# A delta-rule attention and two gated layers on one core: from the third step on, two pairs of small matmul groups are written as one

## The chip, the cores and the metric

The kernel runs on one core of a Trainium2 chip. A core has a matrix engine (TensorE, in the profile PE, with its weight loads as PEld), VectorE (DVE), ScalarE (ACT), GpSimd (POOL) and SyncE (SP, which here only issues DMAs). Each engine runs its own instructions in order, and semaphores tie the engines together. The metric is the device time of one execution in microseconds (us). TensorE's clock is granted by the chip at one of two levels, 2.4 and 1.2 GHz; the profile shows the granted share (1.00 or 0.50, between them where a stretch holds both).

## What is computed

Three layers in a row, all in fp32. The first is a recurrence over 768 positions for 4 x 8 heads of width 48, the second a gated layer (3072 tokens, 384 to 1536 and back), the third sends each token to one of 8 experts. Cut to what matters:

```
for t in range(S):                                   # attention, S = 768
    kt, vt, bt = k_n[:, :, t], v[:, :, t], beta[:, :, t, None]
    y[:, :, t] = einsum('bhd,bhde->bhe', q[:, :, t], state)
    v_old = einsum('bhde,bhd->bhe', state, kt)
    state = state + bt * einsum('bhd,bhe->bhde', kt, vt - v_old)
xn = x / sqrt(mean(x * x) + 1e-6) * rms_g            # second layer
x = (silu(xn @ w_gate) * (xn @ w_val)) @ w_out
e_idx = argmax(x @ gate)                             # third layer: one expert per token
out = gate_w * eom * (relu(x[mask] @ w1[e]) @ w2[e])
```

## The kernel before

**Attention in steps.** The 768 positions are six steps `m` = 0 to 5 of 128, each of two chunks `ch` of 64. The 32 heads are 16 pairs, in two groups `g` of 8 pairs; a step has 32 problems of the form "one head pair's half and one chunk" side by side. In the code the third step is `m` = 2.

`Attn.early(m)` prepares a step for all heads. Small matmuls give the products of keys by keys (`keygram`, L217, tiles `gk`), ScalarE copies them out (L220 to L224), VectorE takes the lengths of the keys into account (`norms`, L135 to L143) after GpSimd has taken square roots (`roots`, L129, tile `nrm`), and `solve` inverts 32 x 32 triangles in 31 rounds of VectorE work (L275, L279). What is left of the 64 x 64 inverse is its corner, in two steps: `corner(m, 0, b)` multiplies raw products by the inverse (L312, tiles `off.0.`), and `corner(m, 1, b)` multiplies the transposed inverse `t11` by what step 0 gave, `w` (L315, tiles `off.1.`). `b` is the half of the 32 problems: a call of `corner` is 32 matmuls of 32 x 32, which the trace counts as 64, and two ScalarE copies out of PSUM (L319 into `w`, L321 into `ng`). The order is step 0 half 0, step 0 half 1, step 1 half 0, step 1 half 1, with a yield behind each.

`Attn.late(m, g)` uses the result. `gram(m, b)` makes keys by queries (L238, tiles `gq`, 16 matmuls of 64 x 64, in the trace 32, and two masked VectorE copies, L245), twice for a group `g`, for `b` = 2g and 2g + 1. Then, for each chunk, four stages: `z` (L335, then a subtraction on VectorE, L339), `u` (L342, then four ScalarE copies, L346), `y` (L357, the output, copied by ScalarE at L362) and `s` (L368, then an addition to the state `right` on VectorE, L371). `z` of the second chunk needs the `right` of the first chunk's `s`.

**The second layer in blocks.** `Moe1.block(m, g)` takes 256 tokens through 12 slices `f`. `up(f)` is 18 fp32r matmuls of 128 x 128 weights by 256 columns into a PSUM tile `gv` (L672; two buffers), then tanh and a copy on ScalarE (L678 `th`, L680 `val`), a product on VectorE (L681), a product on GpSimd (L685), a rounding on ScalarE (L687, `h` high part) and a difference on GpSimd (L688, `h` low part). `down(f - 2)` is 6 matmuls of 400 columns (L698, `po`), which need both parts of `h`. Blocks start with the transposes `xt` (L645) of the scaled input (L634) and end with a route (L725 to L791) that writes the rows to DRAM from SP (L769, L771) and lists tokens by an indirect DMA from GpSimd (L791).

**Third layer.** After the last attention step a plan gathers tokens and weights by indirect DMAs from GpSimd (L833, L986, L993), while the last blocks of the second layer still run.

**What sets the order.** Everything above is written as generators. `Weave` runs the blocks as its main line and steps the attention in between: a generator yields a pair (`pe`, `gap`), TensorE time that it has used and the planned distance to its next turn, and the planner adds `pe` to its own clock. `early` uses `eg` as gap, 3.0 from `m` = 2 on; `late` uses `self.gap`, 3.4 there. A scheduler of the framework then fixes a static order for each engine from these priorities and its own estimate of times. So a changed yield can move instructions on all engines, those of the blocks too.

**Tiles that tie the parts together.** The small products of attention share one PSUM tag, `at`, with four buffers. `t11` lies in the SBUF tag `nb` and `w` in `xa`. The keys of the next step, `ek`, are loaded from SP into the same two tags (L204: group 0 into `nb`, group 1 into `xa`), and the squares of the keys, `sq` (L106), into `xa` and `x`. So the keys of step m + 1 can be loaded only when the last matmul of `corner(m, 1, 1)` has read `t11` and `w`.

Of the kernel before, what the change touches and what calls it, by code (L numbers as in the profile page):

```python
# [29 lines left out]
@contextmanager  # L30
def ahead(tc):

    now, tc.cur_priority = tc.cur_priority, ahead.next
    yield
    ahead.next, tc.cur_priority = tc.cur_priority, now


class Attn:
# [338 lines left out]
    def early(self, m):  # L377


        eg, slow = EGAP[min(m, 2)], SLOW[min(m, 2)]  # L380
        ready = "aT" in self.t[m]
        for g in range(2):
            self.keys(m, 0) if g == 0 else None
            if not ready:
                self.squares(m, g)
            yield 0, 1.0
        self.keys(m, 1)
        T = self.t[m]
        T["raw"] = [self.pool.tile([P, 32, 32], F32, tag=tag, name=f"{tag}r{m}") for tag in ("raw", "x")]
        n = GRAMS.get(m, 0)  # L390
        if n:
            ns = slice(0, 8 * n)
            self.nc.sync.dma_start(out=T["raw"][0][:, ns], in_=self.a["kk", m][:, 0, ns])
            for q in range(4):
                r = slice(32 * q, 32 * q + 32)
                self.nc.sync.dma_start(out=T["raw"][1][r, ns], in_=self.a["kk", m][r, q % 2, ns])
        for g in range(2):
            if 2 * g >= n:
                self.keygram(m, g)
            for b in (2 * g, 2 * g + 1):  # L400
                if not ready:
                    self.roots(m, b)
            yield (0.8 if 2 * g >= n else 0.0), 2 * eg
        if not ready:
            yield 0, 1.0
            self.norms(m)
            yield 0, 1.5
        acc = 0
        solve = self.solve(m)
        while True:  # L410
            with self.behind(m):
                t = next(solve, None)
            if t is None:
                break
            acc += t
            if acc > 0.9:
                yield 0, acc * slow
                acc = 0
        yield 0, acc * slow + 0.5
        for step, b in ((0, 0), (0, 1), (1, 0), (1, 1)):  # L420
            with nullcontext() if m else ahead(self.tc):
                self.corner(m, step, b)
            self.inverted = step == 1 and b == 1
            yield 0.7, eg
        self.solved = m

    def x(self, m, i, xs):
# [32 lines left out]
    def late(self, m, g, xs):  # L460
        T = self.t[m]
        while "aT" not in T:
            yield 0, 1.0
        for b in (2 * g, 2 * g + 1):
            if b < GRAMS.get(m, 0):
                self.mask(m, b)
            else:
                self.gram(m, b)
            yield 0.64, self.gap
        self.values(m, g)  # L470

        while self.solved < m or self.turned < 2 * m - 2 + g:
            yield 0, 1.0
        self.x(m, g, xs)
        for ch in range(2):
            for stage in "zuys":
                if stage == "s" and ch:
                    self.after(m, g, xs[m, g])
                    if m == NM - 1:
                        break  # L480
                self.chain(m, ch, g, stage)
                yield 0.64, self.gap
        if m + 1 < NM:
            for what in "Kqgvk":
                self.load(m + 1, g, what)
# [729 lines left out]
def tile_kernel(ctx: ExitStack, tc: tile.TileContext, a: dict):  # L1215
# [63 lines left out]
    for i in range(PRE):  # L1279
        next(weights)  # L1280
        if i >= GRAMS_AT:
            next(grams, None)
        if i == QUERIES_AT:
            for g in range(2):
                A.load(0, g, "q")
            for _ in range(4):
                next(late)
# [12 lines left out]
    while (0, 0) not in scales:  # L1300
        next(late)
    with ahead(tc):
        for _ in M.turn(0, 0, xs[0, 0]):
            pass
    A.turned = 0
    late = W.add(late)
    W.add(first)
    W.add(weigh(), WSTART)
# [27 lines left out]
    for m in range(NM):  # L1336
# [21 lines left out]
        if m == NM - 2:  # L1358
            for side in [route] + sides:
                W.finish(side)  # L1360
            W.until(lambda: scales[NM - 1, 1] not in W.sides)
            att_s.close()
            p1 = ctx.enter_context(tc.tile_pool(name="c1", bufs=1, side="right"))
            C = Moe2(tc, p1, ps, c, a)
            C.hi[0], C.lo[0] = (p1.tile([P, 3072], F32R, name=f"w1{i}") for i in "hl")

            def early():
                yield from C.plan_full(M.cnt)
                for i in range(2):
                    xg.append(C.gather(p1, *subs[i][1:]))  # L1370
                C.load(subs[0][0], 0)
                C.load(subs[0][0], 1)
                for i in range(2, N1):
                    xg.append(C.gather(p1, *subs[i][1:]))
                yield 0, 14.0
                for i in range(3):
                    C.split(0, i, 3)
                    yield 0, 2.5

            pre = W.add(early())  # L1380
# [103 lines left out]
```

## Time and profile before

| | us |
|---|---|
| median of 3 timed runs | 1078.29 (1073.57 to 1079.56) |
| the profiled execution, its own time | 1081.5 |
| span of the profiled execution, first to last instruction | 1079.7 |
| PE busy | 973.7 (90%), 11189 matmuls |
| PEld busy | 915.5 (85%) |
| DVE busy | 700.0 (65%) |
| ACT busy | 477.1 (44%) |
| POOL busy | 460.6 (43%) |
| mean granted clock of TensorE | 0.977 |

The time line has three parts: a start without full use of TensorE (to about 240 us), the middle, where blocks and attention steps are woven (to about 750 us), and the third layer. The changed calls lie between about 250 and 706 us. In the middle TensorE is busy nearly all the time, so the order there is read from the waits of TensorE and from the granted clock, not from the shares of the whole.

### The profile page before, as it was taken

Reading aid. Unit: us, or ns where it says so; the run is one execution under the profiler, and the core shown is the slowest. Engines: PE = TensorE matmul, PEld = TensorE weight load, DVE = VectorE, ACT = ScalarE, POOL = GpSimd, SP = SyncE. Lnnn points to the kernel's source line nnn. Section 1 sums busy time; section 2 is a strip of 40 time slices with the busy share of each in tenths; the row PEclk is TensorE's granted clock in tenths of the full one; section 3 lists DMA queues with packets and bytes.
Section 4 is the critical chain, followed back from the end, with each engine's and each line's share of the span. In section 5 each row is a group of like instructions: output and inputs, shape, how many; then the busy total and the mean of one; then the engine's idle time right before and its main releaser. Section 6 shows DMA issues by size and latency. Waiting matters only on the chain.

```text
span 1079.7 us, 27699 instructions
## 1 busy us (share of the span) xinstructions
PE 973.7 (90%) x11189; PEld 915.5 (85%) x11189; DVE 700.0 (65%) x1976; ACT 477.1 (44%) x1241; POOL 460.6 (43%) x526
## 2 busy tenths in 40 slices
PE   3825888989999999999999999997998999999993
PEld 2724787889998898989989999997998899999993
DVE  5996879849962898269945995143417756567550
ACT  6625552354345343544364334443335544355440
POOL 9608334443535343543545443346542523324210
PEclk9999999899998999999999999999999999999997
DMA  9811770121302221220222030004106544446320
GB/s 287 236 60 40 207 161 1 30 62 46 74 17 60 60 57 35 61 60 19 58 73 63 2 75 4 14 16 162 66 9 186 203 153 163 154 151 227 144 82 15
DMA packets 55433, 97.05 MB, mean 90 GB/s; under 512 B 6400, under 2 KB 41878, under 8 KB 52482
## 3 DMA queue, kind: packets, MB, share of 16 engines
q1 hardware_dynamic: 45266, 48.76, 17.6%
q0 software_dynamic: 7680, 45.08, 11.7%
q8 instruction: 90, 1.47, 0.6%
q10 hardware_dynamic: 2352, 1.37, 0.5%
q14 instruction: 45, 0.37, 0.1%
HBM read 83.78 MB, written 12.09 MB: 89 GB/s over the span
## 4 chain that ended last, share of the span: by engine, by line
PE 59%; issue 11%; DVE 10%; POOL 7%; DMA 7%; ACT 4%; POOLq 0%; SPq 0%; ACTq 0%; DVEq 0%
PE gv L672 22%; PE po L698 10%; PE cpo L1063 9%; PE ph L1042 8%; PE y L357 2%; POOL th L685 2%; DMA raw<-in_wv_dram 1%; PE gq L238 1%; POOL h L688 1%; POOL nrm L129 1%; DMA sq<-in_kv_dram 1%; POOL raw L560 1%; PE s L368 1%; DVE tmp L275 1%; PE z L335 1%
## 5 line engine op out<-in xcount | busy, mean ns | idle before, releaser
L685 POOL TENSOR_TENSOR th<-th,val 128x256 f32<-128x256 f32 x144 | 115.5, 802 | 249.0 <-DVE th L681 154.9
L698 PE MATMUL po<-wout,h 128*128 128x400 f32 x864 | 191.8, 354 | 10.7 <-POOL h L688 6.5
L681 DVE SCALAR_TENSOR_TENSOR th<-th,gv 128x256 f32<-128x256 f32 x144 | 59.9, 416 | 178.2 <-ACT val L680 167.9
L698 PEld LDWEIGHTS po<-wout,h 128*128 128x128 f32 x864 | 149.2, 190 | 15.8 <-POOL h L688 8.2
L672 PE MATMUL gv<-xh,wl 128*128 128x256 f32 x864 | 151.7, 293 | 3.4 <-DVE th L681 2.1
L672 PE MATMUL gv<-xh,wgv 128*128 128x256 f32 x864 | 147.6, 293 | 2.0 <-DVE th L681 2.0
L688 POOL TENSOR_TENSOR h<-th,h 128x256 fp32r<-128x256 f32 x144 | 110.1, 765 | 82.2 <-ACT h L687 81.6
L687 ACT ACTIVATE h<-th 128x256 fp32r<-128x256 f32 x144 | 60.0, 417 | 192.1 <-POOL th L685 191.0
L672 PEld LDWEIGHTS gv<-xh,wl 128*128 128x128 f32 x864 | 126.2, 195 | 8.6 <-DVE th L681 4.9
L672 PEld LDWEIGHTS gv<-xh,wgv 128*128 128x128 f32 x864 | 124.6, 196 | 5.0 <-DVE th L681 2.7
L1063 PE MATMUL cpo<-w2h,ch 128*128 128x384 f32 (+1 forms) x464 | 124.4, 340 | 3.4 <-ACT ch L1046 3.4
L275 DVE TENSOR_TENSOR tmp<-nb,x 128x110 f32<-128x110 f32 (+35 forms) x366 | 106.8, 331 | 3.7
L678 ACT ACTIVATE th<-gv 128x256 f32<-128x256 f32 x144 | 54.6, 379 | 107.6 <-PE gv L672 92.5
L279 DVE TENSOR_TENSOR x<-x,tmp 128x110 f32<-128x110 f32 (+35 forms) x366 | 98.7, 307 | 0.3
L1042 PE MATMUL ph<-xT,w1h 128*128 128x256 f32 (+4 forms) x528 | 95.1, 313 | 1.1 <-DVE ch L1047 0.8
L1063 PEld LDWEIGHTS cpo<-w2h,ch 128*128 128x128 f32 (+1 forms) x464 | 81.9, 183 | 5.7 <-ACT ch L1046 3.9
L1042 PEld LDWEIGHTS ph<-xT,w1h 128*128 128x128 f32 x528 | 82.4, 190 | 2.7 <-issue 1.6
L672 PE MATMUL gv<-xl,wgv 128*128 128x256 f32 x432 | 80.0, 292 | 0.6 <-DVE xl L653 0.6
L1063 PE MATMUL cpo<-w2l,ch 128*128 128x384 f32 (+1 forms) x232 | 78.1, 337 | 0.0
L672 PE MATMUL gv<-xl,wl 128*128 128x256 f32 x432 | 77.8, 289 | 0.0
L1047 DVE SCALAR_TENSOR_TENSOR ch<-ph,ch 128x512 fp32r<-128x512 f32 (+4 forms) x64 | 39.0, 611 | 45.7 <-ACT ch L1046 45.7
L672 PEld LDWEIGHTS gv<-xl,wgv 128*128 128x128 f32 x432 | 64.4, 196 | 1.7 <-DVE xl L653 1.0
(241 smaller groups left out, 1766.9 us busy)
## 6 DMA issues: line engine op xcount, KB each, us to landing
kT<-in_kqT_dram SPq DMA_DIRECT2D x24, 192.0 KB, 3.8
raw<-in_wo_dram SPq DMA_DIRECT2D x12, 384.0 KB, 7.5
left<-in_kqT_dram SPq DMA_DIRECT2D x24, 192.0 KB, 7.0
v<-in_kv_dram SPq DMA_DIRECT2D x12, 384.0 KB, 3.8
raw<-in_wg_dram SPq DMA_DIRECT2D x12, 384.0 KB, 4.0
raw<-in_wv_dram SPq DMA_DIRECT2D x12, 384.0 KB, 4.1
sq<-in_kv_dram SPq DMA_DIRECT2D x10, 384.0 KB, 4.1
ek<-in_kqT_dram SPq DMA_DIRECT2D x18, 192.0 KB, 3.6
```

The source lines that it names most:

```text
L275: nc.vector.tensor_tensor(out=t, in0=nb[:, k + 1:, k:k + 1].to_broadcast([P, n, b - a]), in1=x[:, k:k + 1, a:b].to_broadcast([P, n, b - a] ...
L279: nc.vector.tensor_tensor(out=x[:, k + 1:, a:b], in0=x[:, k + 1:, a:b], in1=t, op=ALU.add)
L672: nc.tensor.matmul(out=ps[:, gv], lhsT=self.weight(wi, cc, gv, slice(f * P, f * P + P)), rhs=xx[:, cc], start=i == 0, stop=i == 8)
L678: nc.scalar.activation(out=th, in_=ps[:, 0], func=AF.Tanh, scale=0.5)
L681: self.gate = nc.vector.scalar_tensor_tensor(out=th, in0=th, scalar=1.0, in1=ps[:, 0], op0=ALU.add, op1=ALU.mult).ins
L685: nc.gpsimd.tensor_tensor(out=th, in0=th, in1=val, op=ALU.mult)
L687: nc.scalar.activation(out=h2[:, 0], in_=th, func=AF.Copy)
L688: nc.gpsimd.tensor_tensor(out=h2[:, 1], in0=th, in1=h2[:, 0].bitcast(F32), op=ALU.subtract)
L698: nc.tensor.matmul(out=po[t], lhsT=h[:, ts], rhs=self.wo[wi][:, f], start=f == 0 and i == 0, stop=f == 11 and i == 2)
L1042: nc.tensor.matmul(out=ph[:, fl], lhsT=w1[wi][:, cc, f * P:(f + 1) * P], rhs=xt[:, xi, cc], start=i == 0, stop=i == 8)
L1047: nc.vector.scalar_tensor_tensor(out=hl, in0=ph, scalar=0.0, in1=hh.bitcast(F32), op0=ALU.max, op1=ALU.subtract)
L1063: nc.tensor.matmul(out=po[t][0:rows[t]], lhsT=hs[f // 2][:, hi, f % 2, t * P:t * P + rows[t]], rhs=w2[wi][:, f], start=f == 0 and i == 0, ...
```

## The change

From `m` = 2 on, `early` yields only behind half 1 of a corner step, with twice the TensorE time and twice the gap, and `late` yields once behind both products of a group, with twice the time and twice the gap. The calls, the tiles and the instructions are the same; the sums of the planned times are too.

```
@@ in early
             self.inverted = step == 1 and b == 1
-            yield 0.7, eg
+
+            if m < 2:
+                yield 0.7, eg
+            elif b:
+                yield 1.4, 2 * eg
@@ in late
                 self.gram(m, b)
-            yield 0.64, self.gap
+            if m < 2:
+                yield 0.64, self.gap
+        if m > 1:
+            yield 1.28, 2 * self.gap
```

Since the lines behind the edits move by four and then by seven, L672 of before is L679 of the change, and so on.

Three places show what the scheduler makes of it. First TensorE, in block (2, 1), where the corner of step 3 ends (`off310`, `off311` are halves 0 and 1 of its second step). Before:

```order
L315 MATMUL off310_5972<-w3_5820,t113_5700 32x32 x32
L672 MATMUL gv212_6007<-xh21_5808,wgv0_81 128x256 x3
L672 MATMUL gv212_6007<-xl21_5809,wgv0_81 128x256 x3
L672 MATMUL gv212_6007<-xh21_5808,wgv1_82 128x256 x3
L672 MATMUL gv212_6007<-xh21_5808,wgv0_81 128x256 x3
L672 MATMUL gv212_6007<-xl21_5809,wgv0_81 128x256 x3
L672 MATMUL gv212_6007<-xh21_5808,wgv1_82 128x256 x3
L315 MATMUL off311_6035<-w3_5820,t113_5700 32x32 x32
```

Of the change:

```order
L679 MATMUL gv211_5939<-xh21_5879,wgv1_82 128x256 x3
L315 MATMUL off310_5949<-w3_5808,t113_5690 32x32 x32
L315 MATMUL off311_5984<-w3_5808,t113_5690 32x32 x32
L679 MATMUL gv211_5939<-xh21_5879,wgv0_81 128x256 x3
L679 MATMUL gv211_5939<-xl21_5880,wgv0_81 128x256 x3
```

The two halves stand in one run, and the second half has moved ahead of the 18 matmuls of `gv212` and of half of `gv211`.

Second the queue of SP, behind the corner of step 2, in block (1, 1). `y10` are the rows of the route of block (1, 0), `ek0_3` and `ek1_3` the keys and `sq30` and `sq31` the squares for step 3. Before:

```order
L106 DMA sq31_4381<-in_kv_dram 128x768
L769 DMA rows_57<-y10_4008 128x385
L771 DMA rows_57<-y10_4008 64x385 x2
L204 DMA ek0_3_4345<-in_kqT_dram 48x8x128 x2
L106 DMA sq30_4350<-in_kv_dram 128x768
L204 DMA ek1_3_4385<-in_kqT_dram 48x8x128 x2
```

Of the change:

```order
L106 DMA sq31_4381<-in_kv_dram 128x768
L204 DMA ek0_3_4345<-in_kqT_dram 48x8x128 x2
L106 DMA sq30_4350<-in_kv_dram 128x768
L776 DMA rows_57<-y10_4008 128x385
L778 DMA rows_57<-y10_4008 64x385 x2
L204 DMA ek1_3_4385<-in_kqT_dram 48x8x128 x2
```

The loads of `ek0_3` and `sq30` have moved ahead of the rows.

Third GpSimd at the end of the middle part, in block (5, 0): `lt_f` reads the list of tokens, `wraw` are weights of the third layer, `xg` its gathered rows, `th504` to `h506` belong to slices 4 to 6 of the block. Before:

```order
L833 DMA lt_f_10552<-list_60,li_f_10550 6x128
L685 TENSOR_TENSOR th504_10714<-th504_10714,val504_10716 128x256
L993 DMA wraw0_10480<-in_w1_dram,wi_f_10626 128x3072
L993 DMA wraw1_10481<-in_w2_dram,wi_f_10626 128x3072
L688 TENSOR_TENSOR h504_10720<-th504_10714,h504_10720 128x256
L685 TENSOR_TENSOR th505_10748<-th505_10748,val505_10750 128x256
L986 DMA xg0_10628<-rows_57,gi_f_10598 128x385 x2
L986 DMA xg1_10635<-rows_57,gi_f_10598 128x385 x2
L986 DMA xg2_10648<-rows_57,gi_f_10598 128x385 x2
L688 TENSOR_TENSOR h505_10754<-th505_10748,h505_10754 128x256
```

Of the change:

```order
L695 TENSOR_TENSOR h504_10720<-th504_10714,h504_10720 128x256
L840 DMA lt_f_10552<-list_60,li_f_10550 6x128
L1000 DMA wraw0_10480<-in_w1_dram,wi_f_10626 128x3072
L1000 DMA wraw1_10481<-in_w2_dram,wi_f_10626 128x3072
L692 TENSOR_TENSOR th505_10748<-th505_10748,val505_10750 128x256
L692 TENSOR_TENSOR th506_10782<-th506_10782,val506_10784 128x256
L695 TENSOR_TENSOR h505_10754<-th505_10748,h505_10754 128x256
L993 DMA xg0_10628<-rows_57,gi_f_10598 128x385 x2
L993 DMA xg1_10635<-rows_57,gi_f_10598 128x385 x2
L993 DMA xg2_10648<-rows_57,gi_f_10598 128x385 x2
L695 TENSOR_TENSOR h506_10788<-th506_10782,h506_10788 128x256
```

The six gathers now stand behind `h505` and ahead of `h506`, one slice later than before.

## Rows read from the trace of the kernel before

**Rows 1.** Windows: length, busy PE, PEld, DVE, ACT, POOL (count), granted clock, DMA, GB/s

```profile
330.00:340.00 10.00, 8.08 (x120) 7.61 (x121) 2.08 (x6) 5.29 (x15) 9.33 (x8) 0.66 0.31 61
390.00:400.00 10.00, 10.00 (x127) 9.12 (x127) 9.94 (x45) 3.51 (x11) 3.47 (x5) 1.00 0.33 84
460.00:470.00 10.00, 8.73 (x102) 7.84 (x101) 6.65 (x15) 3.65 (x12) 3.87 (x5) 0.83 0.18 42
```

**Rows 2.** Waits of TensorE, 400 to 700 us: us in total, times, longest

```profile
PE z L335 <- DVE right L371: 1.5, 2, 1.3
PE po L698 <- ACT h L687: 1.4, 3, 1.0
PE po L698 <- POOL h L688: 0.5, 3, 0.2
```

**Rows 3.** Timeline of TensorE, block (2, 1): start, us, operation, count

```profile
434.55 0.52 PE L672 MATMUL gv<-xl,wgv 128*128 128x256 f32 x3
434.91 0.52 PE L672 MATMUL gv<-xh,wgv 128*128 128x256 f32 x3
435.36 1.20 PE L315 MATMUL off<-w,t 32*32 32x32 f32 x64
436.49 0.62 PE L672 MATMUL gv<-xh,wgv 128*128 128x256 f32 x3
436.94 0.52 PE L672 MATMUL gv<-xl,wgv 128*128 128x256 f32 x3
```

**Rows 4.** Timeline, corner of step 2 to the keys of step 3; idle in brackets

```profile
324.11 1.20 PE L315 MATMUL off<-w,t 32*32 32x32 f32 x64
...
327.19 0.89 SPq L204 DMA_DIRECT2D ek<-in_kqT_dram  x2
...
330.97 0.41 PE L217 MATMUL gk<-ek 48*64 48x64 f32 x2 [1.64 <-DMA ek<-in_kqT_dram]
332.33 2.08 PE L217 MATMUL gk<-ek 48*64 48x64 f32 x62 [0.95 <-DMA ek<-in_kqT_dram]
...
334.34 1.01 PE L672 MATMUL gv<-xh,wgv 128*128 128x256 f32 x3
...
338.22 0.68 PE L342 MATMUL u<-v,ng 64*64 64x48 f32 x32
```

**Rows 5.** Timeline, what follows in step 2: GpSimd, VectorE, and `z` on TensorE

```profile
339.89 0.73 POOL L685 TENSOR_TENSOR th<-th,val 128x256 f32<-128x256 f32 x1
...
347.84 0.42 DVE L681 SCALAR_TENSOR_TENSOR th<-th,gv 128x256 f32<-128x256 f32 x1 [8.33 <-ACT val L680]
...
351.02 0.32 PE L335 MATMUL z<-right,kT 48*64 48x48 f32 x4
```

**Rows 6.** Timeline, step 3: a wait at the corner, then roots and second `z`

```profile
428.00 0.63 PE L698 MATMUL po<-wout,h 128*128 128x400 f32 x2 [1.02 <-ACT h L687]
...
448.12 6.45 POOL L129 TENSOR_TENSOR nrm<-ss,half 128x8 f32<-128x8 f32 x4
...
457.11 0.77 POOL L685 TENSOR_TENSOR th<-th,val 128x256 f32<-128x256 f32 x1
...
461.74 0.42 DVE L681 SCALAR_TENSOR_TENSOR th<-th,gv 128x256 f32<-128x256 f32 x1 [9.31 <-ACT val L680]
...
462.67 0.39 PE L335 MATMUL z<-right,kT 48*64 48x48 f32 x4 [1.27 <-DVE right L371]
```

**Rows 7.** Timeline, end of the middle part: gathers, `h505`, and TensorE

```profile
741.70 1.04 POOL L986 DMA_INDIRECT xg<-rows,gi_f  x1 [0.16 <-issue]
...
749.90 0.74 POOL L688 TENSOR_TENSOR h<-th,h 128x256 fp32r<-128x256 f32 x1
...
750.69 0.91 PE L698 MATMUL po<-wout,h 128*128 128x400 f32 x2 [5.11 <-POOL h L688]
```

**Rows 8.** Start of block (3, 0): a transpose waits for the scaled input

```profile
490.03 0.52 PE L645 MATMUL xt<-ident,x 128*128 128x128 f32 x3 [0.49 <-DVE x L634]
```

**Rows 9.** ScalarE's copies of corner step 0: count, ns min/median/max, first and last

```profile
L319 ACT ACTIVATE w<-off x24: 571/588/591, 71.2 to 660.8; 32x512 f32<-32x512 f32 x24
```

## Prediction

> **What bounds the kernel now.** I read the windows of 10 us first, then TensorE's waits, then the timeline at each wait. Across the middle part TensorE is busy in nearly all of each window and its clock is at 2.4 GHz; a window like 390 to 400, with TensorE at 10.00 of 10 us and VectorE at 9.94, is the rule while a triangle is inverted, and only two windows of the changed part fall out, 330 to 340 and 460 to 470, where TensorE is busy for 8.08 and 8.73 us and the granted clock is 0.66 and 0.83 [rows 1]. So the order sets the time in two ways: through what TensorE pays for going from one kind of matmul to another, and through a few waits, each of which may cost clock behind it. The waits between 400 and 700 us add up to 1.5 + 1.4 + 0.5 us [rows 2]; ahead of 400 the two waits for the keys of step 3 stand out, and behind 700 the one for `h505`.
>
> **The change part by part.** The instructions are the same; what costs or gains is where they stand.
>
> *Fewer runs.* Three `gv` matmuls take 0.36 us from start to start (434.55 to 434.91); the three ahead of a corner half take 0.45, the half itself 1.13 (435.36 to 436.49), and the three behind it 0.45 again [rows 3]. So an excursion costs 0.09 + 0.09 = 0.18 us beyond its own work. I counted the runs of full-width matmuls between small ones in the two orders: 159 before, 148 in the change. It is not the 15 pairs that the edit joins, because the scheduler still breaks `off2` and `off5` into pieces and joins or breaks other stages. 11 x 0.18 = 2.0 us. Bounds: 0, if VectorE sets the pace where they fall, and 15 x 0.18 = 2.7.
>
> *The keys of step 3.* The last corner half of step 2 runs from 324.11; SP issues `ek0_3` at 327.19, behind the rows of the route; TensorE waits 1.64 and 0.95 us for it, and then runs at half clock: from 334.34 to 338.22 stand 18 `gv` matmuls and nothing else, 3.88 us, where six times 0.36 plus two changes make 2.34 [rows 3, 4]. The 62 `gk` matmuls ahead of them took 2.01 us (332.33 to 334.34) against 1.13 for 64 corner matmuls at full clock. In the change both halves end some 3.5 us earlier, since the 18 `gv` and 6 `po` that lie between them are gone from there (an estimate: 18 x 0.12 = 2.1; 6 of 400 columns in place of 256, 6 x 0.12 x 400 / 256 = 1.1; and 0.2 to 0.3 for the changes), and `ek0_3` and `sq30` stand ahead of the rows in SP's queue. The load took 3.8 us from issue to first use [rows 4], so it lands some 3 us before TensorE comes to it. Gain: 1.64 + 0.95 + (2.01 - 1.13) + (3.88 - 2.34) = 5.0 us.
>
> *What is late next there.* GpSimd's four roots and the listing DMAs still end when they did: `th115` starts on GpSimd at 339.89 [rows 5], and TensorE now comes 5.0 us earlier. In the change ScalarE has `h115` ahead of the copies `x20`, so these, the six copies of `gk31` and then `th116` wait for that: 339.89 + 0.73, + 0.42 for `h115`, + 1.0 for `x20`, + 2.7 for the six, + 0.7 for `th116` and `val116`, + 0.4 and 1.1 on VectorE for `th116` and the state gives about 346.9 for `z210`; it is due at 351.02 - 5.0 = 346.0. I give back 1.0 us. Bounds: 0, and 2.6, if the clock falls behind that wait as it did for 1.6 us behind the keys. (The durations of the copies are estimates from rows of the same shapes, 0.42 us for 128 x 256 on VectorE [rows 5] and 0.59 for a 32 x 512 copy on ScalarE [rows 9].) Net 4.0 us, from 1.4 to 5.0.
>
> *Step 3, the corner.* `po` of `h2011` waits 1.02 us for ScalarE [rows 6]. The second half, 1.13 us, now stands ahead of it and fills the wait. The chain that is waited for ends when VectorE's transposes end, and these stay. Gain 1.0, from 0 to 1.2 (with the small wait behind it).
>
> *Step 3, the second `z`.* The chain is: the four roots, 6.45 us from 448.12, the lists, `th` on GpSimd only at 457.11, ScalarE's queue behind `h`, VectorE's `th215` at 461.74 after 9.31 us of idling, the state, `z` at 462.67 after 1.27 us [rows 6]. In the change the squares' second load and so the roots come some 3.5 us earlier, since `w` is free earlier, and the state's addition stands ahead of `th215` on VectorE, not behind. 1.27 us are gone, and with them the half clock: 1.00 - 0.83 of 10 us is 1.7 us [rows 1]. Gain 3.0, from 0 (if the roots ahead of `th213`, which is their new place on GpSimd, hold ScalarE as long as before) to 3.0.
>
> *Steps 4 and 5.* The rest of [rows 2] is 0.2 + 0.4 + 0.3 us of waits of the same kinds. I take 0.6, from -1 to 0.9.
>
> *Starts of blocks.* `xt301` waits 0.49 us for VectorE's scaling [rows 8], and in the change the scaling of blocks (3, 0) and (5, 0) stands a few VectorE operations later, in (5, 0) behind a stage of attention. I charge 0.5 us each, 1.0 in all, from 0 to 2.0.
>
> *The end of the middle.* TensorE waits 5.11 us for `h505`, which stands on GpSimd behind six gathers that issue from 741.70 to 749.90, 8.2 us [rows 7]. In the change the gathers stand behind `h505` and ahead of `h506`. They start later by `th506` and `h505`, 1.5 us, and some 0.3 us of queue: 743.5 to 751.7, `h506` at 752.4. TensorE has one slice more to do, and comes to `h506` at 750.69 - 5.11 = 745.6 plus 18 `gv` and 6 `po`, 3.5 us: 749.1. The wait is 3.3 and not 5.1, and then 0.2 more for the freed buffer. Gain 1.6, from -1.5 (the plan of the third layer runs late by half a slice) to 5.
>
> *Not moved in cost.* The joined products `gq` need their two buffers at once, and four masked copies follow each other on VectorE; `y`, which reads them, comes a whole stage of attention later, so nothing waits. If that cover is gone, the two more copies cost 1.4 us.
>
> Sum: 2.0 + 4.0 + 1.0 + 3.0 + 0.6 - 1.0 + 1.6 = 11.2 us. The profiled execution took 1081.5 us, so its like would take 1070.3. The median of the timed runs is 3.2 us lower, and the fastest of them 1073.57: some runs seem to have less of these stalls, and less to give. I take half of the 3.2 off: 1069.
>
> **The rivals.**
>
> *The time is set elsewhere, and most is given back.* VectorE is at 9.94 of 10 us in the inversions [rows 1], and GpSimd's roots end when they did in step 2 [rows 5]. If each gain is used up at the next such place, what is left are the changes of run outside the inversions, some 1.2 us, the wait at the corner and part of the tail: 3 us, 1076. For it: the give-back in step 2 is such a case. Against: behind the inversions VectorE is mostly idle, 2.08 of 10 us busy from 330 [rows 1] and 9.31 us without work ahead of `th215` [rows 6], and there the earlier TensorE starts the next inversion earlier too.
>
> *ScalarE's copies become the bound: slower.* A joined corner step leaves four copies in a row on ScalarE, 4 x 0.59 = 2.35 us [rows 9], where there were two. `th` and `val` of the block stand behind them; if TensorE needs their buffer within this, it waits up to 1.18 us at each of 8 corner steps, 9.4 us, and where the clock falls as at 330, 1.6 more: with the gains of the sum cut to the keys and the tail, 1085. It decides from the point where a `gv` buffer is asked for less than 2.35 + 0.8 us after the slice is done. Between the end of one slice and the next but one stand 18 `gv` and 6 `po`, 3.5 us, so it stays just short of that. The Trainium skill, TensorEngine Tiling (Array Packing), PSUM Bottleneck, speaks for this rival: it says that packing small matmuls speeds up TensorE but not the emptying of PSUM, and that the copies may become the bound. By that rule alone the time would be this rival's 1085; the rows show ScalarE at 5.29 us of 10 in the busiest of three windows [rows 1], so I leave it a small chance.
>
> *The stalls are the tail's.* If the gathers find GpSimd free and `h506` comes before TensorE asks for it, the 5.11 us and the half clock behind it go as well: 1063.
>
> *The change does not do what it says.* The scheduler still cuts `off2` and `off5`; if its cuts cost as much as the joined ones save, the first term is 0. That alone moves the time by 2 us and is inside the range.
>
> **How the numbers follow.** The forecast, most terms within their bounds: 0.55, 1064 to 1073, likeliest 1069. Given back: 0.27, 1073 to 1079. Slower by the copies or a wait that I have not seen, with its clock: 0.10, 1079 to 1090. The tail gone as well: 0.08, 1058 to 1064. The range that leaves out no more than 2 in 10 goes from 1062 to 1079. What a measurement of this kernel can tell from no change is about 0.5%, 5.4 us, so faster means below 1072.9: nearly all of the forecast, the last case and a little of the second, 0.65. Within 0.5%: 0.26. Above 1083.7: 0.09.
>
> **What would show it.** Right: no wait of `gk` for `ek` near 325 and a granted clock of 1.00 up to 460; no wait of `z` near 455; a wait of `po` for GpSimd at the gathers of about 3 us, one slice later; runs of 128 corner matmuls in about 2.26 us with one pair of 0.09 around them. Give-back would show as waits of `z` for the state or of `s` for ScalarE in step 2, and of `po` for `h`. Wrong: `gv` waiting for `th` or `val` behind the corner copies, half clock in new windows, or `xt` waiting over 1 us at the starts of blocks (3, 0) and (5, 0).

## The result, and the profile after

The changed kernel takes 1068.72 us (median of 7 runs, 1067.02 to 1069.66), the kernel before 1079.05 (7 runs): a ratio of 0.9909, with a 95% interval from 0.9891 to 0.9928. A later comparison, beside runs of before that took 1082.8 us, gave 0.9911 (0.9883 to 0.9939). Forecast were 1069.0 us, from 1062 to 1079: the time came as forecast, and faster by over 0.5%. Five terms of the sum were off by 0.5 to 1.4 us, a wait that cost 1.5 us stood in no term, and these errors nearly cancel; for the corner of step 3 the reason was wrong as well.

The page of the changed kernel shows the same work in a shorter span (1065.2 us for 1079.7): TensorE is busy for 10.7 us less, with as many matmuls.

```profile
PE 963.0 (90%) x11189; PEld 907.2 (85%) x11189; DVE 705.1 (66%) x1976; ACT 477.8 (45%) x1241; POOL 458.0 (43%) x526
```

The waits of TensorE between 400 and 700 us, which answer to [rows 2] (us in total, times, longest): `z` waits no longer, `po` hardly, and what is left stands at the starts of blocks.

```profile
PE xt L652 <- DVE x L641: 2.2, 4, 1.2
PE po L705 <- ACT h L694: 0.3, 1, 0.3
```

Windows of the changed kernel, with the columns of [rows 1]. In the stretch that answers to 330 to 340 the granted clock is now 1.00; within the middle part it falls only at its end:

```profile
330.00:340.00 10.00, 8.62 (x194) 7.78 (x192) 0.42 (x1) 5.24 (x16) 8.51 (x8) 1.00 0.08 19
...
730.00:740.00 10.00, 6.69 (x52) 6.45 (x50) 2.78 (x3) 3.16 (x6) 8.27 (x10) 0.96 0.91 357
740.00:750.00 10.00, 9.82 (x51) 9.28 (x52) 2.70 (x4) 4.41 (x11) 7.57 (x9) 0.70 0.43 155
```

**Where the time went.** To place it, I compared the start of the same matmul in two traces (TensorE's order is fixed, so the n-th matmul of a family of tiles can be found in both). `gq20` is the first tile at which the two orders differ. It starts at 281.35 us before and at 279.26 after: 2.1 of the 14.5 us between the two spans lie ahead of the change and are not its doing. Behind the last slice another 1.6 us lie in the third layer, whose instructions are the same. What is left is this (us of the start of a slice against the kernel before, both counted from `gq20`; the runs below are explained in the next section):

```
                 gv114   gv200   gv300   gv500   gv510   gv5111
after            -0.18   -4.65   -9.54  -10.56  -10.80  -10.79
corner_only      +0.15   -4.44   -8.81  -10.63  -11.32  -11.32
corner2_only     +0.15   -4.44   -6.95   -7.91  -10.09  -10.09
gram_only        -0.33   -0.15   -0.92   -0.20   -0.83   -0.83
rows_act          0.00   -1.41   -2.47   +0.10   -0.23   -0.23
list_late         0.00   +1.56   -0.65   +3.28   +2.59   +2.59
roots_behind     -0.18   -0.47   -4.45   -3.92   -3.62   -3.61
act_double       -0.17   -3.88   -5.63   -5.20   -5.79   -5.78
tail_spread      -0.10   -4.60   -8.77   -8.30  -12.61   -9.69
after_again      -0.06   -4.53   -8.56   -7.41   -7.79   -7.78
tail_next        -0.18   -4.68   -8.32   -7.62  -13.69  -11.41
corner_again     +0.15   -4.43   -7.98   -8.86   -8.93   -8.93
corner_tail_next +0.15   -4.46   -7.92   -9.21  -16.46  -14.56
```

`gv114` follows the corner of step 2, `gv200` opens block (2, 0) behind the keys of step 3, `gv300` follows step 3, and the six gathers of the tail lie between `gv500` and `gv510`. The last 10.8 us fit the 10.3 us between the medians. From list_late down, the runs were measured later, beside slower runs of before, and there some runs of small matmuls stall (last section). Their traces are compared with the one trace of before that there is, from the first measurement.

### The profile page after: what moved, and what is told of

Read it like the earlier page. It is cut to its first block, busy times and chain, and to the rows that moved or that the text cites. A ratio compares the mean times of both kernels' runs of the same rounds, so it can differ in the third digit from the quotient of the medians.

```text
span 1065.2 us, 27702 instructions
## 1 busy us (share of the span) xinstructions
PE 963.0 (90%) x11189; PEld 907.2 (85%) x11189; DVE 705.1 (66%) x1976; ACT 477.8 (45%) x1241; POOL 458.0 (43%) x526
## 4 chain that ended last, share of the span: by engine, by line
PE 61%; issue 10%; DVE 10%; POOL 8%; DMA 5%; ACT 3%; ACTq 0%; SPq 0%; POOLq 0%; DVEq 0%
PE gv L679 23%; PE po L705 11%; PE cpo L1070 9%; PE ph L1049 9%; PE y L357 2%; POOL th L692 2%; POOL raw L567 1%; DVE x L279 1%; DVE tmp L275 1%; PE s L368 1%; PE z L335 1%; PE u L342 1%; PE gq L238 1%; POOL nrm L129 1%; POOL h L695 1%
## 5 line engine op out<-in xcount | busy, mean ns | idle before, releaser
L692 POOL TENSOR_TENSOR th<-th,val 128x256 f32<-128x256 f32 x144 | 113.2, 786 | 248.3 <-DVE th L688 148.3
L679 PE MATMUL gv<-xh,wl 128*128 128x256 f32 x864 | 148.3, 290 | 3.3 <-DVE th L688 3.2
L679 PE MATMUL gv<-xh,wgv 128*128 128x256 f32 x864 | 145.3, 289 | 2.2 <-DVE th L688 1.8
L679 PEld LDWEIGHTS gv<-xh,wl 128*128 128x128 f32 x864 | 124.7, 193 | 7.9 <-DVE th L688 6.1
L679 PEld LDWEIGHTS gv<-xh,wgv 128*128 128x128 f32 x864 | 121.7, 192 | 5.4 <-DVE th L688 2.6
L275 DVE TENSOR_TENSOR tmp<-nb,x 128x110 f32<-128x110 f32 (+35 forms) x366 | 110.9, 342 | 3.6
L679 PE MATMUL gv<-xl,wgv 128*128 128x256 f32 x432 | 78.3, 287 | 0.7 <-DVE xl L660 0.7
L679 PE MATMUL gv<-xl,wl 128*128 128x256 f32 x432 | 77.2, 286 | 0.0
L679 PEld LDWEIGHTS gv<-xl,wgv 128*128 128x128 f32 x432 | 63.0, 192 | 1.6 <-DVE xl L660 1.1
```

The costliest lines, as they stand in the source:

```text
L275: nc.vector.tensor_tensor(out=t, in0=nb[:, k + 1:, k:k + 1].to_broadcast([P, n, b - a]), in1=x[:, k:k + 1, a:b].to_broadcast([P, n, b - a] ...
L679: nc.tensor.matmul(out=ps[:, gv], lhsT=self.weight(wi, cc, gv, slice(f * P, f * P + P)), rhs=xx[:, cc], start=i == 0, stop=i == 8)
L692: nc.gpsimd.tensor_tensor(out=th, in0=th, in1=val, op=ALU.mult)
```

## Experiments

The kernel before took 1079.2 us beside the runs up to rows_act, 1083.4 beside the next four and 1082.8 beside the last four. The first two of these groups ran on chip 12, the last on chip 2; why before is slower in the second and third is not known. So the ratios are to be compared, not the times.

**corner_only, gram_only, corner2_only: which part of the change.** Each leaves out a part of the edit:

```
corner_only:  late yields 0.64, self.gap behind each product, as before
gram_only:    early yields 0.7, eg behind each half, as before
corner2_only: as corner_only, and in early
-            if m < 2:
+            if m != 2:
```

> Only the halves of a corner step are joined from the third step on; the products of keys by queries yield one by one as before. By place (each gain belongs to the call that stands beside it): the keys of step 3 give 4.4 us, the corner and the second z of step 3 together 5, the fewer runs of the corner 1, and the wait of u at 389 in the change (1.4 us with its lost turn) has no reason to stand: 1068 to 1071, no wait of gk for ek. By reshuffling (the whole order moved, and what came of it is chance): no relation to the change, anywhere from 1070 to 1083, with the 1.27 us wait of z at 463 or the 1.02 us wait of po at 428 still there although the corners are joined.

> Only the two products of keys by queries of a group are joined from the third step on; the corner halves yield one by one as before. By place: six runs of full-width matmuls fewer than before (145 for 151 between small ones), 6 x 0.18 = 1.1 us, and the waits for the keys (1.64 and 0.95 us), at the corner of step 3 (1.02) and at its second z (1.27) all stay: 1077 to 1079. By reshuffling: several of these waits go or others come, 1069 to 1075 or over 1082.

> Only the halves of the corner steps of the third step (m = 2) are joined. By place: the waits for the keys of step 3 go with the half clock behind them, 6.1 us, of which 1.4 to 1.7 are given back by the next wait in that step: 1074 to 1075.5, and the waits at 428 and 463 of before stay. By give-back (GpSimd's roots set that stage): the two waits go, but a wait of z for the state takes 4 us or more: 1077 to 1079.

Measured: corner_only 1066.3 us, ratio 0.9889 (0.9864 to 0.9913); gram_only 1077.99, 0.9996 (0.9974 to 1.0018); corner2_only 1072.13, 0.9938 (0.9916 to 0.996). What is left at the end is the corners' gain; joining the products alone gives nothing that can be measured, and the two waits of gram_only for the keys of step 3 stand as before (1.72 and 0.98 us; the third wait in this row is for the keys of step 4, and new):

```profile
PE gk L217 <- DMA ek<-in_kqT_dram: 3.3, 3, 1.7
```

But the waits at the corner of step 3 and at its second `z`, which I expected to stay in gram_only, did not. Its waits of TensorE from 400 to 500 us:

```profile
PE xt L648 <- DVE x L637: 1.5, 2, 1.0
PE gk L217 <- DMA ek<-in_kqT_dram: 0.6, 1, 0.6
PE po L701 <- ACT h L690: 0.2, 1, 0.2
```

The 1.02 us of `po` have become 0.2, and the wait of `z` and the half clock behind it are gone, with no corner joined. By the starts of the same matmuls 1.9 us are gained at that corner and 3.2 at that `z`, and 4.2 are given back: at `u` in step 2 (1.0), between the corner and the `z` (1.8), and ahead of block (3, 0) (1.4). So the account of this run by place was right in its time (1077 to 1079 forecast) and wrong in its waits.

corner2_only, too, shows that not all gains are where I had put them. With only the corner of step 2 joined, the waits at 428 and 463 should have stayed, and both are gone:

```profile
PE xt L649 <- DVE x L638: 1.7, 2, 1.0
PE z L335 <- DVE right L371: 0.5, 1, 0.5
PE po L702 <- ACT h L691: 0.2, 1, 0.2
```

(Waits of TensorE from 400 to 700 us.) The timeline of the corner of step 3 in corner2_only (start, us, engine, operation) shows why, at the place of [rows 6], 428.00:

```profile
416.32 1.97 DVE L294 STREAM_TRANSPOSE ng<-xa 32x1024 f32<-32x1024 f32 x1
...
418.15 0.39 DVE L685 SCALAR_TENSOR_TENSOR th<-th,gv 128x256 f32<-128x256 f32 x1
...
418.57 1.99 DVE L294 STREAM_TRANSPOSE ng<-xa 32x1024 f32<-32x1024 f32 x1
...
420.90 2.43 PE L702 MATMUL po<-wout,h 128*128 128x400 f32 x10
```

Before, both transposes stood in one piece (4.01 us) ahead of `th` on VectorE, and `h2011` came late. Here `th` stands between them, and ten `po` follow one corner half without a wait. The changed kernel has the same order:

```profile
416.71 0.39 DVE L688 SCALAR_TENSOR_TENSOR th<-th,gv 128x256 f32<-128x256 f32 x1
417.13 1.98 DVE L294 STREAM_TRANSPOSE ng<-xa 32x1024 f32<-32x1024 f32 x1
```

So has gram_only (transposes at 422.83 and 425.29, `th` at 424.83). In corner2_only and gram_only no second half stands at that place to fill a wait, and the wait is gone or nearly so; what the three orders share is `th` between the transposes. A run with this swap alone was not made. Why the scheduler moved VectorE's order is not shown; in gram_only it did so with no corner changed.

**rows_act: was it SP's queue?** The kernel before, with three row writes of one route on another queue:

```
+            dma = nc.scalar if (m, g) == (1, 0) else nc.sync
-            nc.sync.dma_start(out=rows[m * P:(m + 1) * P, 2 * g], in_=y[:, 0])
+            dma.dma_start(out=rows[m * P:(m + 1) * P, 2 * g], in_=y[:, 0])
...
```

> The kernel before, with the three row writes of the route of block (1, 0) issued from ScalarE's queue in place of SP's; the order of every other instruction is the same. It asks how much of the wait for the keys came from SP's queue and how much from the late corner half. By the queue: ek is issued when the corner's last half ends, about 325.4 in place of 327.2, 1.8 us earlier; the first wait of 1.64 us goes, the second of 0.95 shrinks or goes, and the half clock behind them with them: 1074 to 1075. By the corner half alone: the load cannot start before the half has been read, waits of 1 us and the half clock stay, 1077 to 1079.

Measured: 1076.66 us, ratio 0.9978 (0.996 to 0.9996). Counted from `gq20`, `ek` was issued when I expected it, and the first wait went. The second grew to 1.55 us, and the second group of keys, for which TensorE did not wait before, now costs 0.92:

```profile
322.27 0.84 SPq L204 DMA_DIRECT2D ek<-in_kqT_dram  x2
...
327.92 1.76 PE L217 MATMUL gk<-ek 48*64 48x64 f32 x62 [1.55 <-DMA ek<-in_kqT_dram]
...
338.82 1.16 PE L217 MATMUL gk<-ek 48*64 48x64 f32 x62 [0.92 <-DMA ek<-in_kqT_dram]
```

That is 2.47 us of waiting for 2.59; the stretch at half clock behind it is shorter (granted clock 0.92 from 320 to 330 and 0.91 from 330 to 340, so 1.7 us are lost, where 0.66 in one window cost 3.4). At `gv200` it is 1.4 us ahead, against 4.4 to 4.7 with the corner of step 2 joined. So moving the rows off SP's queue gives less than a third of that term by itself. The earlier corner half with the rows still ahead of `ek` was not tried, so how the rest divides is open. Further on, the same order on TensorE as before met the half clock at other places: behind the 1.01 us wait of `po` at 423.55 (granted clock 0.83 from 424 to 434) and behind a wait of 1.10 us of `z` at 572, and nothing of the gain is left at the last slice.

**list_late and roots_behind: GpSimd's order.** Two swaps of one product with what stands ahead of it on GpSimd: in the kernel before, `th214` ahead of the two listing DMAs of block (2, 0); in the changed kernel, `th115` ahead of the last two roots of step 3.

```
list_late:
         for t in range(2):
+            with self.tc.issue_after(self.mul[1]) if (m, g) == (2, 0) else nullcontext():
...
roots_behind:
+                    with self.tc.issue_after(self.mul()) if m == 3 and g else nullcontext():
                         self.roots(m, b)
```

> The kernel before, with one swap on GpSimd: th214 stands ahead of the two listing DMAs of block (2, 0) in place of behind them; every other engine has the order of before. By GpSimd's order (what was late for the second z of step 3 is th behind roots and lists, whatever the corners do): th214 starts at about 454.8 in place of 457.1, the wait of z at 462.67 (1.27 us) goes, and with it the half clock behind it (1.7): 1076 to 1076.5. By the corner (only joined halves bring the roots early enough): the wait of z stays at 0.8 us or more, 1078 to 1080.

> The changed kernel, with one swap on GpSimd: th115 stands ahead of the last two roots of step 3 in place of behind them; every other engine has the order of the change. If the wait of s at 339.14 (1.38 us) is what was given back behind the keys, it goes, since th115, h115 and then the copies x20 come 3.3 us earlier: 1067.3. If the roots are late themselves for the norms and the low half of h115 for po, the wait only moves: 1068 to 1069.5.

Both expectations say that the other engines keep their order. That is not so for ScalarE: the scheduler also moved the copy `h214` ahead of the two copies `x30`, and `h115` ahead of the four copies `right` of the same stage. The other engines did keep theirs.

list_late: 1080.6 us, ratio 0.9979 (0.9949 to 1.0009); in time that cannot be told from no change. In the trace the wait of `z` is gone and the clock is whole, with nothing done to any corner:

```profile
454.62 0.72 POOL L685 TENSOR_TENSOR th<-th,val 128x256 f32<-128x256 f32 x1
...
455.52 1.06 POOL L794 DMA_INDIRECT list<-tok,pos  x1 [0.18 <-issue]
...
463.16 0.32 PE L335 MATMUL z<-right,kT 48*64 48x48 f32 x4
```

Between `gv200` and `gv300` it gains 2.2 us (+1.56 to -0.65), in spite of a stall of 0.37 us that the first runs do not have. So `th` behind the lists, with what ScalarE then ran ahead of `h214`, was what made `z` late; corner2_only and gram_only have `th` ahead of the lists as well. The time was lost again at 569 to 575, in three stalls of 0.38 us in `gk` and at half clock behind them.

roots_behind: 1074.42 us, ratio 0.9923 (0.9901 to 0.9946), no gain. The wait of `s` is gone, but a larger one stands ahead of it, and the clock falls (0.66 from 335 to 345), so that 4.2 us are lost by `gv200`:

```profile
335.76 0.42 ACT L695 ACTIVATE h<-th 128x256 fp32r<-128x256 f32 x1 [2.75 <-POOL th L693]
...
336.20 1.38 ACT L346 ACTIVATE right<-u 64x192 f32<-64x192 f32 x4
336.58 0.32 PE L357 MATMUL y<-right,left 128*64 128x48 f32 x2 [2.18 <-ACT right L346]
```

The swap on GpSimd came with one on ScalarE: `h115`, which waits for `th115` behind a root and the lists, now held `right`, for which `y` waits. Both theories that I had written miss it.

**act_double: are the copies of the corner the bound?** The changed kernel, with each of these copies made twice from the third step on:

```
-                nc.scalar.activation(out=w[o, ns], in_=ps[o], func=AF.Copy)
+                for _ in range(1 if m < 2 else 2):
+                    nc.scalar.activation(out=w[o, ns], in_=ps[o], func=AF.Copy)
...
```

> The changed kernel with every copy of a corner step on ScalarE made twice from the third step on (8 copies of 0.59 us in a row where there were 4). If ScalarE's copies are near the point where they set the time, as the rival of the prediction says (4.7 + 0.8 us against the 3.5 us between two slices), th and val of the slice wait, and gv of the next but one waits up to 2 us at each of the 8 corner steps: 1073 to 1085. If there is room, because few corner steps meet a slice at that moment, 1069 to 1071.

Measured: 1074.87 us, ratio 0.9924 (0.9892 to 0.9956), which cannot be told from the 0.9909 of the change. The wait that the rival names appears, at two of the eight corner steps, with 0.71 and 0.73 us; the first is this:

```profile
428.72 4.23 ACT L323 ACTIVATE ng<-off 32x512 f32<-32x512 f32 x7
...
434.21 0.61 PE L681 MATMUL gv<-xh,wgv 128*128 128x256 f32 x3 [0.71 <-DVE th L690]
```

The four copies more held ScalarE some 2.35 us longer and TensorE waited for 0.7 of it. So at that step the changed kernel had some 1.6 us to spare (an estimate). A wait of `gk` for `v`, 0.68 us at 438.68, which the changed kernel does not have, came behind it.

**tail_spread, tail_next, corner_tail_next: the gathers.** The six gathers are issued one by one, each behind the low half of `h` of one slice, in block (5, 0) or in block (5, 1):

```
                 C.load(subs[0][0], 1)
-                for i in range(2, N1):
-                    xg.append(C.gather(p1, *subs[i][1:]))
+                gathers = W.add(spread())
...
+                        while M.low[0] < (NM - 1, 0, f):      # tail_next: (NM - 1, 1, f)
+                            yield 0, 0.3
...
+            with self.tc.issue_after(behind()):
+                self.nc.gpsimd.indirect_dma_start(
...
```

> The changed kernel, with the six gathers of the third layer's first tokens issued one by one behind the low halves of slices 4 to 9 of block (5, 0), in place of six in a row between h505 and h506. If the wait of po for h506 (3.31 us) and the half clock behind it (6.8 us at half, 3.4 us lost) are both the gathers' doing, both go: 1068.7 - 6.7 = 1062. If the clock falls there for another reason, or the third layer gives it back: 1065 to 1069.

> The changed kernel, with the six gathers one by one behind the slices of block (5, 1), 50 us later than in the change, so that no block border lies behind them. If the gathers cost the 3.31 us of po and half of the 6.8 us at half clock, and the spread over slices 4 to 9 only pushed the wait to the border of the blocks, then 5 to 6.7 us are gained: 1062 to 1064, or 0.983 to 0.986 of before. If the third layer waits for the gathered rows in their place, 1067 to 1070.

> Corner halves joined, products of keys by queries not, gathers one by one behind the slices of block (5, 1): both of the last two together. If they add up, 1060 to 1063 (0.981 to 0.985 of before); if the gathers' new places move the wait, as corner_again.

tail_spread: 1070.2 us, ratio 0.9883 (0.9828 to 0.9937). At the place of the gathers 5.1 us are gained over the changed kernel, and 3.9 of them are lost within 10 us, at the border to block (5, 1), whose input `xh` is now late on ScalarE. From 750 to 760 the granted clock is 0.83. The two longest waits of TensorE from 720 to 760 us:

```profile
PE po L706 <- ACT h L694: 1.0, 1, 1.0
PE gv L679 <- ACT xh L659: 0.8, 1, 0.8
```

tail_next: 1071.33 us, ratio 0.9899 (0.9873 to 0.9925). The clock stays at 1.00 from 730 to 760, and from `gv500` to `gv510` the kernel gains 6.1 us (-7.62 to -13.69) where the changed kernel gains 0.2. Of this 2.3 are lost again in block (5, 1) itself, and the third layer takes another 3.2 in a wait of its own, so in time nothing can be told:

```profile
784.68 0.63 PE L706 MATMUL po<-wout,h 128*128 128x400 f32 x2 [1.52 <-POOL h L695]
...
855.17 3.56 PE L1063 MATMUL ph<-xT,w1h 128*128 128x432 f32 x9 [3.22 <-ACT xT L1039]
```

corner_tail_next: 1067.57 us, ratio 0.9868 (0.9839 to 0.9897). Its interval overlaps that of the changed kernel beside it, 0.9911 (0.9883 to 0.9939), but both go by the same runs of before. Compared directly, its five runs average 1067.8 us and the changed kernel's six 1073.4: 5.6 us less, with a 95% interval of about 2.2 to 8.9. So it is likely to beat the changed kernel, though not by the amount I expected of it; in the trace it keeps 5.6 us over corner_again at the last slice. Five runs on one chip are few.

**after_again and corner_again.** The changed kernel and corner_only once more, beside these two on one chip.

> The changed kernel once more, beside the three below on one chip: 0.989 to 0.993 of the kernel before, with the waits of its first profile (s 1.38, u 0.86, xt 1.17, po 3.31 us).

> The corner halves joined, the products of keys by queries not, once more. If joining the products is worth nothing, as the anchors in the two traces say (10.8 and 11.3 us ahead of before at the last slice), within 0.3% of the changed kernel. If it costs what the medians say (1066.3 against 1068.7), 0.2 to 0.4% below it.

Measured: 0.9911 and 0.9903 (0.9879 to 0.9928). The waits of the first profile were there again (1.39, 0.87, 1.17 and 3.83 us, the last half a microsecond longer). Joining the products is worth nothing that these measurements can see, in either direction.

## Why the prediction came out right

**Fewer runs (2.0).** The change runs both halves as one. TensorE around the second corner step of step 3, which answers to [rows 3]:

```profile
425.45 0.52 PE L679 MATMUL gv<-xh,wgv 128*128 128x256 f32 x3
425.90 2.21 PE L315 MATMUL off<-w,t 32*32 32x32 f32 x128
428.05 0.62 PE L679 MATMUL gv<-xh,wgv 128*128 128x256 f32 x3
428.50 0.52 PE L679 MATMUL gv<-xl,wgv 128*128 128x256 f32 x3
```

From the first to the last of these starts pass 3.05 us. Two halves apart would take twice 2.03 (434.91 to 436.94 in [rows 3]) less the two triples of `gv` that are counted twice, 0.72: 3.34. So a joined pair saves 0.29 us here, not 0.18; 64 corner matmuls cost 1.07 in the long run and 1.13 alone. The sum over all runs could not be measured apart from the waits between them: gram_only has six runs fewer and is 0.83 us ahead at the last slice, where 1.1 were expected.

**The keys of step 3 (4.0 net).** 4.5 us (-0.18 to -4.65), and the two parts are as the prediction put them: more gained, and then given back at `s` rather than at `z`. The timeline that answers to [rows 4] and [rows 5]:

```profile
317.56 2.08 PE L315 MATMUL off<-w,t 32*32 32x32 f32 x118
...
319.67 1.66 SPq L204 DMA_DIRECT2D ek<-in_kqT_dram  x2
...
326.80 1.13 PE L217 MATMUL gk<-ek 48*64 48x64 f32 x64
...
334.29 3.29 POOL L129 TENSOR_TENSOR nrm<-ss,half 128x8 f32<-128x8 f32 x2
...
337.55 0.72 POOL L692 TENSOR_TENSOR th<-th,val 128x256 f32<-128x256 f32 x1
...
338.30 0.42 ACT L694 ACTIVATE h<-th 128x256 fp32r<-128x256 f32 x1 [4.58 <-POOL th L692]
...
339.14 0.92 PE L368 MATMUL s<-right,k 64*48 64x48 f32 x32 [1.38 <-ACT x L362]
```

The load lands well ahead, and 64 `gk` take 1.13 us at full clock. Then the step that I had named as late next is late: GpSimd ends its roots, `th115` follows at 337.55, `h115` and the copies `x20` behind it. TensorE meets this at `s`, which waits 1.38 us for `x20`, one stage ahead of the `z` that I had looked at. The gain ahead of it was 6.1 us in place of 5.0 (a `gv` of slice 114 starts 2.38 us earlier than in the trace before, one of slice 116 8.45), because the half clock had held for longer than the two rows that I costed (3.4 us lost by the 0.66 of [rows 1], of which I had 2.4). corner2_only, with only this corner joined, gains as much (+0.15 to -4.44), and gram_only nothing, so this term is where I had put it.

**Step 3, the corner (1.0).** 2.4 us, twice its upper bound of 1.2: the `po` that ran ahead of it at 422.78 starts 5.93 us earlier than before, a `gv210` behind it (431.94 before) 8.29. The number holds the wait of 1.02 and 0.18 us, and three breaks of the corner that are gone (two pieces of four matmuls and the half itself). The step that failed is the reason. I wrote that the second half fills the wait and that VectorE's transposes stay. The transposes did not stay: `th` stands between them, and corner2_only and gram_only, which have that order and no second half there, have no wait or 0.2 us of it. gram_only gains 1.9 us at this place without the edit at the corner.

**Step 3, the second `z` (3.0).** 3.0 us (8.28 to 11.32), no wait at `z`, and a whole clock. GpSimd, VectorE and TensorE, which answer to [rows 6]:

```profile
435.15 6.44 POOL L129 TENSOR_TENSOR nrm<-ss,half 128x8 f32<-128x8 f32 x4
441.56 0.74 POOL L692 TENSOR_TENSOR th<-th,val 128x256 f32<-128x256 f32 x1
442.46 1.06 POOL L798 DMA_INDIRECT list<-tok,pos  x1 [0.17 <-issue]
...
447.45 1.14 DVE L371 TENSOR_TENSOR right<-right,s 48x384 f32<-48x384 f32 x2 [3.64 <-PE s L368]
...
450.90 0.32 PE L335 MATMUL z<-right,kT 48*64 48x48 f32 x4
```

The roots are earlier, as forecast, and the state's addition waits for nothing but `s`. But `th` also stands ahead of the lists here and behind them before, and list_late shows that this swap, without earlier roots, is enough for the wait and the clock; gram_only, with the same swap, gains 3.2 us here with no corner joined. So the number was right, and the earlier corner, from which I had it, was not needed for it.

**What the sum left out: `u` in step 2 (-1.5).** The prediction's rival of gains given back in the inversions has a case here, at a place that no term covered:

```profile
384.04 0.67 PE L335 MATMUL z<-right,kT 48*64 48x48 f32 x28
...
388.37 0.34 DVE L339 TENSOR_TENSOR v<-v,z 128x192 f32<-128x192 f32 x1
...
388.76 1.12 PE L342 MATMUL u<-v,ng 64*64 64x48 f32 x32 [0.86 <-DVE v L339]
```

VectorE is busy for 9.87 of the 10 us from 380. It comes to the subtraction `v` 3.7 us after the end of `z` (384.71 to 388.37), behind rounds of the inversion and steps of a route; before, it was 2.0 us (392.45 to 394.42), with as many matmuls between `z` and `u`. So `u` waits 0.86 us and takes 0.4 longer than its 0.68: a `gv` ahead of it starts 6.78 us earlier than before, one behind it 5.32. I had expected the wait to go in corner_only; it stands there (0.87 us, and 0.93 at another `u`, at 610.42) and in corner2_only (0.87), and gram_only has 0.58, so neither part of the edit is its only cause.

**Steps 4 and 5 and the starts of blocks (0.6 - 1.0).** From `gv300` to `gv500` 1.0 us is gained, where the two terms together gave -0.4; runs saved in these steps are in the number. The transposes of blocks wait more, as forecast: block (3, 0), just ahead of `gv300`, for 1.17 us at 478.07 where [rows 8] has 0.49. That is over the 1 us that I had named as a sign of being wrong; block (5, 0) waits 0.28.

**The end of the middle (1.6).** 0.2 us (-10.56 to -10.80). The order and the wait were right to a tenth of a microsecond (3.3 forecast), which the rows that answer to [rows 7] show:

```profile
730.90 1.04 POOL L993 DMA_INDIRECT xg<-rows,gi_f  x1 [0.18 <-issue]
...
739.17 0.73 POOL L695 TENSOR_TENSOR h<-th,h 128x256 fp32r<-128x256 f32 x1
...
739.95 1.03 PE L705 MATMUL po<-wout,h 128*128 128x400 f32 x2 [3.31 <-POOL h L695]
```

The term was mis-sized because I let the clock behind the wait stay as it was. Before, 0.17 of a window of 10 us were lost to it (0.83 from 750 to 760, so 1.7 us); after, 0.30 and 0.04 (0.70 and 0.96 in the windows above), 3.4 us. Here the shorter wait cost more clock, but that does not go with the order. In after_again, the same kernel, the wait is 3.83 us and 1.7 us of clock are lost behind it, and from `gv500` to `gv510` it gains 0.4 us:

```profile
740.00:750.00 10.00, 6.26 (x31) 5.93 (x32) 2.70 (x4) 4.06 (x10) 8.71 (x10) 0.83 0.36 109
```

So the term is worth 0.2 to 0.4 us in two profiles, and how much of that is the clock changes between them.

**The rivals.** ScalarE's copies: not the bound. The Trainium skill, TensorEngine Tiling (Array Packing), PSUM Bottleneck, says that copying out of PSUM may become the bottleneck once tiling has made TensorE faster. Here, with four copies in a row, no `gv` waits for them, and with eight two corner steps of eight make one wait, for 0.7 us. Given back: true at `s` and `u`, 2.8 us in all, not for most of the gain. The tail gone: it did not go by itself. Where it was taken away, the border of the blocks (tail_spread) or block (5, 1) and the third layer (tail_next) took most of it back; corner_tail_next kept some 5 us.

So the sum came out (11.2 us, against 10.8 at the last slice and 10.3 in the medians) because its errors cancel. More was gained than forecast at the keys (0.5 us), at the corner (1.4) and in steps 4 and 5 with the starts of blocks (1.4). Less was gained by the tail (1.4) and by the fewer runs (what lies outside the places named is 1.1 us, where 2.0 were forecast for all runs), and `u` took 1.5. The mechanism at the keys was right: an earlier load, and then GpSimd late for the stage behind it. That the hit is so close is luck.

## What to carry to other kernels

Where a scheduler sets the order, an edit at one stage moves the order of engines at later stages; undo the edit there, and try each part of it alone and look at its waits and not only its time, before you believe that it acts there. For a stalled load, ask for the last reader of its buffer as well as for the queue that issues it: here the queue by itself gave less than a third. Compare two traces by the starts of the same instruction, from the first that differs, so that what the run did ahead of it is not counted as the change.

## What the hardware showed

Whether the clock falls behind a wait does not follow from the length of the wait alone. In the changed kernel, the wait of 1.38 us at 339.14 was followed by a whole clock; in rows_act a wait of 1.01 us at 423.55 was followed by half clock, where the kernel before, with the same order and 1.02 us ([rows 6], 428.00), has a whole one. At the gathers the same kernel lost 3.4 us of clock behind a wait of 3.31 us in one profile and 1.7 behind 3.83 in the other. The windows of 10 us around the waits at 339.14 and 423.55, in this order:

```profile
335.00:345.00 10.00, 8.62 (x149) 7.53 (x142) 1.44 (x3) 5.23 (x16) 4.96 (x6) 1.00 0.01 2
```

```profile
424.00:434.00 10.00, 9.85 (x175) 9.28 (x174) 2.81 (x10) 4.49 (x11) 1.77 (x3) 0.83 0.05 16
```

So a term for the clock behind a wait of one to two microseconds belongs in the range, 0 to 1.7 us, and not in the sum.

In the runs from list_late on TensorE stalls inside runs of small matmuls (`gk`, at times `s`), for nothing that the profile shows; list_late, whose TensorE order is that of before, has 1.1 us of it in `gk` between 400 and 700 us (the row below) and 0.4 in `s`, and the kernel before none:

```profile
PE gk L217 <- issue: 1.1, 3, 0.4
```

after_again has two of them (0.40 us at 444.89, 0.36 at 560.34) and is 7.8 us ahead of the first profile of before at the last slice and not 10.8; its ratio, beside runs of before on the same chip, is the same. Between `gv200` and `gv500` its granted clock is whole, so the 3 us are not lost to the clock; the stalls themselves and the waits of `z` behind the second (0.49 us) are part of them, and the rest was not placed. What causes the stalls was not tried.
